# Interleaving the first batch's down tiles by halves of the contraction

## The chip, the cores and the metric

One core of one Trainium2 chip runs the whole program. The metric is the device time of that core in microseconds (us), lower is better. One run of a kernel has a profile; the other runs have a time and a mean granted clock alone (the share of full speed at which TensorE was let run). The times of a run are about 1.8 us longer than the span that its profile shows.

## The reference

```python
# q: 8 x 16 x 384 x 64, k and v: 8 x 4 x 384 x 64 (4 query heads share a key head)
attn = softmax(q @ k.T / sqrt(64)) @ v           # per batch and head
x = attn.transpose(0, 2, 1, 3).reshape(3072, 1024)
h = maximum(x @ w_in, 0)                         # w_in 1024 x 2048
out = (h * h) @ w_out                            # w_out 2048 x 1024, float32
```

The change touches only the last product, and of it only the 384 tokens of the first batch.

## The kernel before

The kernel works through 8 batches of 384 tokens. TensorE is given attention work of the next batch in between the feed-forward work of this one. A list scheduler, which runs when the kernel is built and has a clock of its own, fixes the order of the instructions on each engine. On the chip each engine then goes through its list in order and waits at semaphores.

The feed-forward has an "up" stage (x times w_in) and a "down" stage (times w_out). A down tile is 128 tokens by 512 output columns in one PSUM bank (6 or 7). Its contraction of 2048 is 16 matmuls of 512 columns, given out as four parts of 4. There are two column halves (`jj`) and three token blocks (`i3`), so six tiles a batch.

```python
    def load_w_out(jj, part):      # a quarter of w_out: column half jj, row half part
        R.add("gpsimd", lambda g: g.dma_start(
            w_out_sb[:, 8 * part:8 * part + 8, jj * 512:(jj + 1) * 512],
            moe_w_out[part * 1024:(part + 1) * 1024, jj * 512:(jj + 1) * 512]
            .rearrange("(c p) f -> p c f", p=128)),
            writes=[("w_out", jj, part)], dma=f"wo{jj}{part}", cost=5.3, issue=0.9)
    # ... (the eight loads of w_in are issued first, then:)
    for jj in range(2):
        for part in range(2):
            load_w_out(jj, part)
```

```python
    def ffn(b):
        # ... the up stage
        for jj in range(2):
            for i3 in range(NJ):                                     # NJ = 3
                # ... (the very last tile is cut in two)
                    at = []
                    for part in range(4):
                        yield down_part(b, jj, i3, c0, c1, part, at)

    def down_part(b, jj, i3, c0, c1, part, at):
        n = c1 - c0

        def piece():
            if part == 0:
                at.append(pick((6, 7)))
            i = at[0]

            def mm(pe):
                for c in range(4 * part, 4 * part + 4):
                    m = pe.matmul(bank(i)[:, 0:n], h2T[b % 2][:, c, i3 * 128:(i3 + 1) * 128],
                                  w_out_sb[:, c, c0:c1], start=(c == 0), stop=(c == NFC - 1))
                return m

            R.add("tensor", mm, reads=need, writes=[("bank", i)], cost=4 * (n / 2400 + 0.0025))
            # ... after part 3: DVE copies the bank to y_sb, SyncE stores it
        need = [("w_out", jj, part // 2)] + [("h2T", b % 2, c) for c in range(4 * part, 4 * part + 4)]
        return 0, need, (6, 7) if part == 0 else None, piece
```

Parts 0 and 1 need w_out's first row half, parts 2 and 3 its second. In the old order the second half is wanted after only 8 matmuls.

The softmax here doesn't subtract the row's maximum and nothing guards it: scores larger than these inputs give would overflow.

Of the kernel before, what the change touches and what calls it, by code (L numbers as in the profile page):

```python
# [136 lines left out]
def bass_gqa_attention__then__ffn_squared_relu_kernel(  # L137
# [13 lines left out]
    NJ = S // 128  # L151
# [38 lines left out]
    def bank(i):  # L190
        return ps[:, i, :]
# [4 lines left out]
    def pick(allowed):  # L196
        turn_count[0] += 1
        i = min(allowed, key=lambda i: (max(R.when(writes=[("bank", i)]), R.clock["tensor"]), used[i]))
        used[i] = turn_count[0]
        return i  # L200
# [226 lines left out]
    def up_part(b, c, at, k0, k1, banks=(6, 7)):  # L427
        def piece():
            if k0 == 0:
                at.append(pick(tuple(banks)))  # L430
                held.add(at[0])
            i = at[0]
            if k1 == NKC:
                held.discard(i)

            def mm(pe):
                for kc in range(k0, k1):
                    m = pe.matmul(bank(i)[:, 0:S], w_in_sb[:, kc, c * 128:(c + 1) * 128],  # L438
                                  xT[b % NXT][:, kc, :], start=(kc == 0), stop=(kc == NKC - 1))
                return m  # L440

            R.add("tensor", mm, reads=need, writes=[("bank", i)], cost=0.1625 * (k1 - k0))
            if k1 == NKC:
                r = hr_n[0] % NHR
                hr_n[0] += 1
                R.add("vector", lambda e: e.tensor_scalar_max(hr[r][:, :], bank(i)[:, 0:S], 0.0),  # L446
                      reads=[("bank", i)], writes=[("hr", r)], cost=0.48)
                R.add("scalar", lambda e: e.activation(h2T[b % 2][:, c, :], hr[r][:, :], AF.Square),  # L448
                      reads=[("hr", r)], writes=[("h2T", b % 2, c)], cost=0.42)

        need = [("w_in", c * 128 // WC)] + [("xT", b % NXT, kc) for kc in range(k0, k1)]
        return k1, need, banks if k0 == 0 else None, piece
# [10 lines left out]
    def ffn(b):  # L463

        for c in range(0 if b else EARLY, NFC):
            at = []
            for k0 in (0, 4):
                yield up_part(b, c, at, k0, k0 + 4)
        for jj in range(2):
            for i3 in range(NJ):  # L470
                last = b == B - 1 and (jj, i3) == (1, NJ - 1)
                for c0, c1 in ((512, 896), (896, 1024)) if last else ((512 * jj, 512 * jj + 512),):
# [19 lines that stand above are left out]
            if part == 3:  # L492
                yb = y_n[0] % (2 * NY)
                y_n[0] += 1
                ysl = y_sb[yb // 2][:, (yb % 2) * 512:(yb % 2) * 512 + n]
                R.add("vector", lambda e: e.tensor_copy(ysl, bank(i)[:, 0:n]),  # L496
                      reads=[("bank", i)], writes=[("y", yb)], cost=0.08 + n / 960)
                rows = out[b * S:(b + 1) * S, :].rearrange("(p j) f -> j p f", j=NJ)[i3]
                R.add("sync", lambda e: e.dma_start(rows[:, c0:c1], ysl),
                      reads=[("y", yb)], writes=[("out", b, i3, c0)], dma=f"y{yb}", cost=1.0)  # L500
                stored.append(("out", b, i3, c0))

        need = [("w_out", jj, part // 2)] + [("h2T", b % 2, c) for c in range(4 * part, 4 * part + 4)]
        return 0, need, (6, 7) if part == 0 else None, piece
# [90 lines left out]
    def feed():  # L595
        for b in range(B):
            for item in ffn(b):
                yield (b,) + item
# [9 lines left out]
    while av_q or av_open or sc_q or o_q or f_head is not None:  # L608
# [18 lines left out]
        if turn_q:  # L627
            b, g, w = turn_q[0]
# [5 lines left out]
        elif av_q:  # L634
            b, c = av_q[0]
# [5 lines left out]
        if sc_q:  # L641
            b, u = sc_q[0]
            if b == 0:
                tiles = {(0, x, t) for x, c0, n in smalls[u] for t in range(c0 // 128, (c0 + n) // 128)}
# [14 lines left out]
        for n, lane in enumerate(lanes):  # L659
            chunks, need, banks, _ = lane[0]  # L660
# [7 lines left out]
        if f_head is not None and not lanes:  # L668
            b, chunks, need, banks, piece = f_head
# [15 lines left out]
        if what[2] == "turn":  # L685
            b, g, w = turn_q.pop(0)
# [5 lines left out]
        elif what[2] == "av":  # L692
            b, c = av_q.pop(0)
            av_open = (b, c, av(b, c, spare))
            next(av_open[2])
        elif what[2] == "av2":
            b, c, rest = av_open
# [8 lines left out]
        elif what[2] == "o":  # L706
            b, c, _ = o_q.pop(0)
            turn_o_pe(b, c, spare)
            x_done[b] += 1
        elif what[2] == "sc":  # L710
            b, u = sc_q.pop(0)
# [44 lines left out]
```

## Time and profile before

The kernel takes 429.41 us (median of 3 runs, 429.10 to 429.62).

| of the profile before | |
|---|---|
| span | 427.2 us |
| TensorE busy | 421.9 us, 99% |
| second-busiest compute engine (ACT) | 194.2 us, 45% |
| TensorE waits on w_out | one, 1.1 us |

From the page of the kernel before (PE is TensorE, PEld its weight loads, DVE VectorE, ACT ScalarE, POOL GpSimd): busy time of TensorE with its share and instructions, the DMA busy tenths in 40 slices, the shares of the chain that ended last, the group of the down matmuls (busy us, mean ns of one, then idle time before them), and the loads of w_out (KB each, median us from issue to landing).

```profile
PE 421.9 (99%) x3462; PEld 231.6 (54%) x3462; DVE 157.9 (37%) x333; ACT 194.2 (45%) x194; POOL 55.2 (13%) x67
...
DMA  9999999999499469539919310063001100110012
...
PE 87%; DMA 10%; POOL 2%; issue 0%; DVE 0%; POOLq 0%
...
L487 PE MATMUL ps<-w_out_sb,h2T 128*128 128x512 bf16 (+2 forms) x784 | 172.3, 375 | 1.1 <-DMA w_out_sb<-in_moe_w_out_dram 1.1
...
w_out_sb<-in_moe_w_out_dram POOLq DMA_DIRECT2D x4, 1024.0 KB, 30.6
```

TensorE is the limit, so only its idle time can be won. The DMA engines are busy over 90% in the first ten slices (107 us), and the chain goes through DMA for 10% of the span. The chain is followed back from the end, so it meets the last wait before which TensorE depended on a transfer: the load of w_out.

All waits of TensorE in the kernel before (who, for what, us in total, times, longest):

```profile
PE ps L487 <- DMA w_out_sb<-in_moe_w_out_dram: 1.1, 1, 1.1
PE ps L545 <- DVE v_aug L540: 1.1, 1, 1.1
PE ps L309 <- DMA q_st<-in_q_dram: 0.4, 1, 0.4
PE ps L309 <- DVE qT L316: 0.2, 1, 0.2
```

L545 is the warm-up and L309 the turning of the first queries: start-up work. Only the first line is in the steady part. Its place is seen in the timeline of TensorE before (start us, us, engine, line, operation, what, count, and in brackets the idle time before it):

```profile
51.06 1.89 PE L487 MATMUL ps<-w_out_sb,h2T 128*128 128x512 bf16 x8
54.06 1.04 PE L487 MATMUL ps<-w_out_sb,h2T 128*128 128x512 bf16 x4 [1.11 <-DMA w_out_sb<-in_moe_w_out_dram]
54.94 1.28 PE L381 MATMUL ps<-v_aug,expT 128*128 128x65 bf16 x36
56.05 1.89 PE L487 MATMUL ps<-w_out_sb,h2T 128*128 128x512 bf16 x8
57.87 0.82 PE L356 MATMUL ps<-qT,kT 64*128 64x512 bf16 x8
...
76.17 5.36 PE L438 MATMUL ps<-xT,w_in_sb 128*128 128x384 bf16 x32
81.46 0.82 PE L356 MATMUL ps<-qT,kT 64*128 64x512 bf16 x8
```

Eight matmuls run (parts 0 and 1 of the first tile), then TensorE stands still until the second row half has landed. L381 is an attention-value group and L356 are scores of the next batch. A busy span's modelled end overhangs the start of the next matmul, so idle time is better counted from start to start: 8 matmuls at 0.216 us fill 51.06 to 52.79, and the next starts at 54.06. That is 1.27 us lost, a little more than the 1.11 in brackets.

### The profile page before, as it was taken

How to read it: one execution, taken by the hardware profiler on the slowest of the kernel's cores; microseconds unless marked ns; L12 is line 12 of the kernel's file. 1: busy time of each engine (PE TensorE's matmuls, PEld its weight loads, DVE VectorE, ACT ScalarE, POOL GpSimd, SP SyncE). 2: the span in 40 equal slices, each digit the busy share in tenths (PEclk: the TensorE clock that was granted, in tenths of full speed). 3: DMA queues.
4: the chain of work that ended last, by engine and by line, in shares of the span. 5: the costliest groups of instructions: out<-in, count | busy, mean ns of one | idle time of the engine just before them, and what ended most of it. 6: DMA issues, size and time to landing. Idle time of an engine off the chain costs nothing.

```text
span 427.2 us, 7835 instructions
## 1 busy us (share of the span) xinstructions
PE 421.9 (99%) x3462; PEld 231.6 (54%) x3462; DVE 157.9 (37%) x333; ACT 194.2 (45%) x194; POOL 55.2 (13%) x67
## 2 busy tenths in 40 slices
PE   8999999999999999999999999999999999999997
PEld 5665554555545555455554455555564465446544
DVE  3664332343423443234442244343441144214412
ACT  6957720477256773547745477732230033003300
POOL 8680001414012004004000000000000000000000
PEclk9999999999999999999999999999999999999999
DMA  9999999999499469539919310063001100110012
GB/s 172 194 186 201 185 202 217 201 174 151 92 201 164 32 130 123 126 88 153 106 45 180 87 45 18 2 104 93 27 2 49 74 26 1 51 74 26 1 66 82
DMA packets 96915, 44.30 MB, mean 104 GB/s; under 512 B 77296, under 2 KB 90864, under 8 KB 96880
## 3 DMA queue, kind: packets, MB, share of 16 engines
q0 software_dynamic: 36544, 17.44, 32.4%
q1 hardware_dynamic: 59664, 25.86, 29.5%
q8 instruction: 27, 0.44, 0.4%
q10 hardware_dynamic: 672, 0.49, 0.4%
q14 instruction: 8, 0.07, 0.0%
HBM read 35.65 MB, written 12.58 MB: 113 GB/s over the span
## 4 chain that ended last, share of the span: by engine, by line
PE 87%; DMA 10%; POOL 2%; issue 0%; DVE 0%; POOLq 0%
PE ps L487 39%; PE ps L438 35%; PE ps L381 7%; DMA w_out_sb<-in_moe_w_out_dram 7%; PE ps L356 7%; DMA v_st<-in_v_dram 4%; POOL q_st L237 1%; POOL w_in_sb L247 1%; POOL v_aug L269 0%; POOL w_out_sb L253 0%; DVE y_sb L496 0%; POOL ident L513 0%; POOL ident L512 0%; POOLq L513 0%; POOLq L741 0%
## 5 line engine op out<-in xcount | busy, mean ns | idle before, releaser
L438 PE MATMUL ps<-xT,w_in_sb 128*128 128x384 bf16 x1024 | 175.0, 326 | 0.0
L487 PE MATMUL ps<-w_out_sb,h2T 128*128 128x512 bf16 (+2 forms) x784 | 172.3, 375 | 1.1 <-DMA w_out_sb<-in_moe_w_out_dram 1.1
L366 ACT ACTIVATE expT<-ps 128x3072 bf16<-128x3072 f32 x42 | 114.4, 2724 | 64.6 <-PE ps L356 64.0
L438 PEld LDWEIGHTS ps<-xT,w_in_sb 128*128 128x128 bf16 x1024 | 97.1, 98 | 69.6 <-issue 6.2
L448 ACT ACTIVATE h2T<-hr 128x384 bf16<-128x384 f32 x128 | 64.3, 520 | 143.0 <-DVE hr L446 143.0
L487 PEld LDWEIGHTS ps<-w_out_sb,h2T 128*128 128x128 bf16 x784 | 73.6, 98 | 88.6 <-issue 5.1
L446 DVE TENSOR_SCALAR hr<-ps 128x384 f32<-128x384 f32 x128 | 71.3, 557 | 106.5 <-PE ps L438 106.5
L496 DVE COPY y_sb<-ps 128x512 f32<-128x512 f32 (+2 forms) x49 | 33.4, 681 | 124.0 <-PE ps L487 124.0
L381 PEld LDWEIGHTS ps<-v_aug,expT 128*128 128x128 bf16 x1152 | 39.9, 97 | 6.8 <-DVE rinv L390 0.5
L381 PE MATMUL ps<-v_aug,expT 128*128 128x65 bf16 x1152 | 41.8, 193 | 0.0
L396 DVE TENSOR_TENSOR o_sb<-ps,rinv 128x384 bf16<-128x384 f32 x64 | 35.7, 558 | 2.2
L356 PE MATMUL ps<-qT,kT 64*128 64x512 bf16 (+1 forms) x336 | 34.6, 325 | 0.0
L356 PEld LDWEIGHTS ps<-qT,kT 64*128 64x128 bf16 x336 | 13.0, 94 | 20.4 <-issue 5.7
L390 DVE RECIPROCAL rinv<-ps 128x6 f32<-128x6 f32 x64 | 12.2, 190 | 26.7 <-PE ps L381 26.7
L269 POOL COPY v_aug<-v_st 128x768 bf16<-128x768 bf16 x8 | 6.6, 828 | 86.7 <-PE ps L381 69.9
L345 ACT ACTIVATE expT<-ps 128x1024 bf16<-128x1024 f32 (+1 forms) x20 | 16.8, 991 | 1.0 <-PE ps L335 1.0
L264 POOL COPY k_dup<-k_st 128x1536 bf16<-128x1536 bf16 x7 | 10.3, 1467 | 42.3 <-DMA k_st<-in_k_dram 42.1
L237 POOL DMA_DIRECT2D q_st<-in_q_dram x17 | 14.9, 888 | 0.3 <-issue 0.2
L205 POOL DMA_DIRECT2D k_st<-in_k_dram x7 | 5.3, 764 | 37.9 <-DMA qT<-q_st 37.9
L335 PE MATMUL ps<-qT,kT 64*128 64x384 bf16 (+2 forms) x48 | 7.3, 334 | 0.1
L247 POOL DMA_DIRECT2D w_in_sb<-in_moe_w_in_dram x8 | 7.1, 900 | 0.0
L230 POOL DMA_DIRECT2D v_st<-in_v_dram x8 | 6.3, 789 | 0.0
(27 smaller groups left out, 41.9 us busy)
## 6 DMA issues: line engine op xcount, KB each, us to landing
out_dram<-y_sb SPq DMA_DIRECT2D x47, 256.0 KB, 2.0
q_st<-in_q_dram POOLq DMA_DIRECT2D x14, 384.0 KB, 8.6
w_in_sb<-in_moe_w_in_dram POOLq DMA_DIRECT2D x8, 512.0 KB, 14.6
w_out_sb<-in_moe_w_out_dram POOLq DMA_DIRECT2D x4, 1024.0 KB, 30.6
v_st<-in_v_dram POOLq DMA_DIRECT2D x8, 192.0 KB, 10.3
k_st<-in_k_dram POOLq DMA_DIRECT2D x7, 192.0 KB, 4.4
q_st<-in_q_dram POOLq DMA_DIRECT2D x3, 192.0 KB, 6.1
xT<-o_sb SPq DMA_TRANSPOSE x28, 3.9
```

What stands on the lines that cost most here:

```text
L237: R.add("gpsimd", lambda g: g.dma_start(q_st[st][:, h0:h1, :], q[b, h0:h1].rearrange("h (p j) d -> p h (j d)", j=NJ)), writes=[("q_st", st ...
L345: R.add("scalar", lambda e: e.activation(dst, src, AF.Exp, scale=0.125), reads=keys, writes=[("expT", (b * NU + u) % NEX, t) for u, _, _ i ...
L356: m = pe.matmul(flat[:, k0 * HC + c0:k0 * HC + c1], kT[b % 2][64 * x:64 * x + 64, u + k0, :], q_cols(b, (u + k0) // NJ, x, c0, c1))
L366: R.add("scalar", lambda e: e.activation(dst, src, AF.Exp, scale=0.125), reads=keys, writes=[("expT", (n + m) % NEX, t) for m in range(2) ...
L381: m = pe.matmul(po[:, f - 6 * s2, 0:D + 1], w, v_aug[b % 2][:, g * NJ + j, 0:D + 1], start=(j == 0), stop=(j == NJ - 1))
L390: R.add("vector", lambda e: e.reciprocal(rinv[r].ap().unsqueeze(2), po[:, :, D:D + 1]), reads=[("bank", i)], writes=[("rinv", r)], cost=0.13)
L396: R.add("vector", lambda e: e.tensor_tensor(dst, srcv, rbv, ALU.mult), reads=[("bank", i), ("rinv", r)], writes=[("o_sb", o, s2)], cost=0.48)
L438: m = pe.matmul(bank(i)[:, 0:S], w_in_sb[:, kc, c * 128:(c + 1) * 128], xT[b % NXT][:, kc, :], start=(kc == 0), stop=(kc == NKC - 1))
L446: R.add("vector", lambda e: e.tensor_scalar_max(hr[r][:, :], bank(i)[:, 0:S], 0.0), reads=[("bank", i)], writes=[("hr", r)], cost=0.48)
L448: R.add("scalar", lambda e: e.activation(h2T[b % 2][:, c, :], hr[r][:, :], AF.Square), reads=[("hr", r)], writes=[("h2T", b % 2, c)], cost ...
L487: m = pe.matmul(bank(i)[:, 0:n], h2T[b % 2][:, c, i3 * 128:(i3 + 1) * 128], w_out_sb[:, c, c0:c1], start=(c == 0), stop=(c == NFC - 1))
L496: R.add("vector", lambda e: e.tensor_copy(ysl, bank(i)[:, 0:n]), reads=[("bank", i)], writes=[("y", yb)], cost=0.08 + n / 960)
```

## The change

The intent is to read w_out's second row half later. In batch 0 token blocks 0 and 1 first do their parts 0 and 1, in two banks, and then their parts 2 and 3. Block 2 follows alone. Sixteen down matmuls then stand before the first read of the second half. No instruction is added or removed, and batches 1 to 7 keep their code.

```diff
-        for jj in range(2):
+        for jj in range(2 if b == 0 else 0):
+            ats = [[] for _ in range(NJ)]
+            for tiles in ((0, 1), (2,)):
+                for half in range(2):
+                    for i3 in tiles:
+                        for part in (2 * half, 2 * half + 1):
+                            yield down_part(b, jj, i3, 512 * jj, 512 * jj + 512, part, ats[i3])
+        for jj in range(2 if b else 0):
```

## The prediction

> **What bounds the kernel now.** TensorE. The busy table gives PE 421.9 of 427.2 us (99%) at full granted clock; ACT 45%, DVE 37%. Matmuls stream: late in the chain view 96 down matmuls of 512 columns take 20.72 us, 216 ns each. The Trainium skill ("TensorE: Matmul & The Clock Gate", "Back-to-back issue gap") gives 512 columns at 2.4 GHz plus 2.5 ns, also 216 ns; the trace agrees. So only PE idle time can be won. The waits view filtered to PE has four waits: 1.1, 0.4 and 0.2 us in the lead-in, and one later: 1.1 us of the down matmuls on w_out.
>
> **That wait.** In the PE timeline batch 0's down tiles begin at 51.06 us with eight matmuls (parts 0 and 1 of tile 0, on w_out's first row half). The third part, on the second half, starts at 54.06 us. The four w_out loads, issued at 24.8 to 27.4 us, land 23.1, 28.4, 32.9 and 38.2 us later: at about 47.9, 54.0, 59.4 and 65.6 us, one per 5.7 us, behind each other on DMA engines that the page shows over 90% busy. Eight matmuls fill their slots until 51.06 + 1.73 = 52.79 us. Lost, start to start: 1.27 us (the view shows 1.1, as a modelled end overhangs its slot).
>
> **What the change does.** No instruction is added or removed. In batch 0 come parts 0 and 1 of tiles 0 and 1, then parts 2 and 3 of both, then tile 2. Sixteen matmuls (3.46 us) precede the first read of the second half, so it comes no sooner than 54.5 us, and 1.1 us later if an attention-value group (36 matmuls, 1.12 us) falls between, as one now does after the third part. Slack after landing: 0.4 to 1.5 us. The wait should vanish.
>
> In the second column half nothing is to be gained: its second row half is now read at about 67.5 us, 1.9 us after landing.
>
> **Costs.** Two banks are open at once, so an eviction (0.69 us) must fit into the other tile's two parts (1.73 us). It does, closely if DVE has an attention group too (about 1.3 us). The first store comes 1.7 us later, with no reader.
>
> **Does the gain survive?** After 54 us PE never waits in the trace, so the saving goes through unless a DMA becomes the limit. The nearest: batch 2's first scores start at 81.46 us; their query transpose, issued at 72.30, landed 7.8 us later, about 80.1. Shifted, the scores start at 80.2: just in time; a few tenths may be lost.
>
> **Prediction.** 429.4 - 1.27 = about 428.2 us (0.3%); 8 in 10 between 427.7 and 429.0. Faster by over 2%: 1%; within 2%: 98%; slower by over 2%: 1%.
>
> **What would show it right.** No PE wait on w_out; the first second-half matmul at 54.5 to 56 us; batch 1's first up matmuls at about 74.9 us instead of 76.17; the last down group 1.27 us earlier (404.16 to 402.9); PE busy time unchanged; w_out landings unchanged within 0.5 us.
>
> **What would make it wrong.** A new PE wait: on the query transpose at batch 2's first scores, on an eviction when a bank is reused, or still on w_out if it lands later than in the recorded run. The order of later work is fixed at build time by a list scheduler with its own clock, so a moved tile can reshuffle attention work of batches 1 and 2 and make or remove waits of about 1 us. A bank chosen wrongly there would show as a wrong result, not as time.

## The result, and the profile after

| | median us | range | runs |
|---|---|---|---|
| before, same rounds | 429.25 | 428.53 to 429.75 | 6 |
| after | 427.84 | 427.56 to 427.95 | 6 |

The ratio is 0.9966 with a 95% interval of 0.9953 to 0.9979: a gain of 0.34%, small but clear of noise. A ratio is always the mean time of one kernel's fast runs over that of the other's of the same rounds, so it is not quite the ratio of the medians. The output is correct. The runs after also lie closer together: 0.39 us from end to end against 1.22 us.

From the page after, the lines that answer to those of before:

```profile
PE 422.2 (99%) x3462; PEld 231.9 (54%) x3462; DVE 157.9 (37%) x333; ACT 194.4 (46%) x194; POOL 55.2 (13%) x67
...
DMA  9999999999989369449829310053001100110012
...
PE 97%; DMA 1%; DVE 0%; ACT 0%; issue 0%; POOL 0%; POOLq 0%
...
L494 PE MATMUL ps<-w_out_sb,h2T 128*128 128x512 bf16 (+2 forms) x784 | 172.1, 375 | 0.0
...
w_out_sb<-in_moe_w_out_dram POOLq DMA_DIRECT2D x4, 1024.0 KB, 30.8
```

The work is the same (the down matmuls are now L494; the 0.3 us more of TensorE busy time lie in the first 10 us, 8.60 against 8.30, before anything that the change touches). The idle time before them went from 1.1 to 0.0, and the chain no longer passes through the load: its DMA share fell from 10% to 1%. Such a share is not the size of a gain. The chain had 10% on DMA, and removing that wait gave 0.34%, because behind it stood TensorE work that was nearly as long.

All waits of TensorE after:

```profile
PE ps L552 <- DVE v_aug L547: 1.1, 1, 1.1
PE ps L309 <- DVE qT L316: 0.2, 1, 0.2
```

The timeline of TensorE after:

```profile
51.08 2.75 PE L494 MATMUL ps<-w_out_sb,h2T 128*128 128x512 bf16 x12
53.67 1.28 PE L381 MATMUL ps<-v_aug,expT 128*128 128x65 bf16 x36
54.78 1.89 PE L494 MATMUL ps<-w_out_sb,h2T 128*128 128x512 bf16 x8
56.60 0.82 PE L356 MATMUL ps<-qT,kT 64*128 64x512 bf16 x8
...
74.90 5.36 PE L438 MATMUL ps<-xT,w_in_sb 128*128 128x384 bf16 x32
80.28 0.82 PE L356 MATMUL ps<-qT,kT 64*128 64x512 bf16 x8
```

The sequence of kinds and counts is the same: 12 down matmuls, an attention-value group, 8 down matmuls, scores. On every engine the two kernels' lists have the same instructions in the same order by shape. Only which tile and part a down matmul belongs to has changed, so the scheduler has not reshuffled anything. The first read of the second half is now the second four of the eight at 54.78, at 55.65 us. The next up stage begins 1.27 us earlier (76.17 to 74.90), as much as the idle time that was removed (the down stage itself began 0.02 us later). At the scores of batch 2 the distance from there is 5.29 us before and 5.38 after: 0.09 us were given back (0.01 in the profile of the next series, 75.02 to 80.32). The weight loads there now have a wait of 0.4 us on the transposed queries, which landed at 80.24. This is the line of the waits view after:

```profile
PEld ps L356 <- DMA qT<-q_st: 0.4, 1, 0.4
```

The gain then stays to the end. The last piece of down matmuls in the chain, first before, then after:

```profile
404.16 20.77 PE ps L487 x112
```

```profile
402.98 20.77 PE ps L494 x112
```

That is 1.18 us, which is 1.27 less 0.09.

### The profile page after: what moved, and what is told of

It reads as the page before. It is cut to its first block, busy times and chain, and to the rows that moved or that the text cites. A ratio compares the mean times of both kernels' runs of the same rounds, so it can differ in the third digit from the quotient of the medians.

```text
span 426.0 us, 7835 instructions
## 1 busy us (share of the span) xinstructions
PE 422.2 (99%) x3462; PEld 231.9 (54%) x3462; DVE 157.9 (37%) x333; ACT 194.4 (46%) x194; POOL 55.2 (13%) x67
## 4 chain that ended last, share of the span: by engine, by line
PE 97%; DMA 1%; DVE 0%; ACT 0%; issue 0%; POOL 0%; POOLq 0%
PE ps L438 40%; PE ps L494 39%; PE ps L381 9%; PE ps L356 7%; DMA q_st<-in_q_dram 1%; PE ps L335 1%; PE ps L309 1%; PE ps L414 0%; PE ps L292 0%; ACT expT L345 0%; DVE qT L316 0%; DVE y_sb L503 0%; POOL ident L520 0%; POOL ident L519 0%; POOLq L520 0%
## 5 line engine op out<-in xcount | busy, mean ns | idle before, releaser
L494 PE MATMUL ps<-w_out_sb,h2T 128*128 128x512 bf16 (+2 forms) x784 | 172.1, 375 | 0.0
L494 PEld LDWEIGHTS ps<-w_out_sb,h2T 128*128 128x128 bf16 x784 | 73.7, 98 | 87.2 <-issue 5.1
```

## The experiments

Theory W: the gain is the wait for w_out's second row half and nothing else. Rival V: it is the new order as such (two banks in turn, evictions and stores spaced differently). In all the kernels below the lists of all engines except GpSimd are the same by shape as before, so that only the named thing differs. The exception is the pair with the early key load, in which SyncE's list differs too (the key transpose comes one store earlier); the two kernels of that pair have the same lists as each other. Edits of kernels in the new order are shown against the changed kernel, the others against the kernel before.

The table has the places that decide, from each trace: when w_out's second part (second row half of column half 0) and fourth part (of column half 1) landed, and when the first matmul that needs it started.

| kernel | 2nd part landed | read | 4th part landed | read |
|---|---|---|---|---|
| before | 54.02 | 54.06 | 65.59 | 67.53 |
| after | 54.85 | 55.65 | 67.11 | 67.99 |
| after, again | 54.95 | 55.77 | 67.20 | 68.12 |
| only column half 0 | 54.93 | 55.82 | 66.34 | 66.44 |
| only column half 1 | 54.87 | 54.91 | 66.05 | 70.12 |
| no wait, wrong data | 54.54 | (58.06) | 66.99 | 67.04 |
| one part between | 54.00 | 54.89 | 65.97 | 67.24 |

Where a read stands some 0.05 us after a landing, TensorE was waiting for it. (In the kernel with wrong data the first tile doesn't read the second part; 58.06 is the first read of it, by the second tile.)

### The change again

No edit.

> The changed kernel again, as the mark for the other runs of this chip. Theory W (the gain is the wait for w_out's second row half, and nothing else): 1.0 to 1.8 us under the kernel before, near 427.8, no PE wait on w_out. Rival V (the gain is the new order as such: two banks alternating, evictions and stores spaced otherwise): the same here.

Measured: 427.63 us (427.51 to 427.89, 5 runs) against 429.55 (428.82 to 430.33, 11 runs) of the kernel before on this chip, ratio 0.9960 (0.9948 to 0.9972). No wait on w_out. The gain is confirmed, here 1.9 us between the medians.

### Only column half 0

```diff
-        for jj in range(2 if b == 0 else 0):
+        for jj in range(1 if b == 0 else 0):
...
-        for jj in range(2 if b else 0):
+        for jj in range(0 if b else 1, 2):
```

> Only the first column half is interleaved. W: all of the gain, within 0.3 us of the changed kernel (427.8), no PE wait on w_out; the second column half's reads come after their landings anyway. V: about half of the gain, near 428.5.

Measured: 427.94 us, ratio 0.9973 (0.9957 to 0.9988), 6 runs from 427.71 to 429.45. By the median W holds. But two runs stand apart, at 428.30 and 429.45, where the whole change has none above 427.95. In the profiled run the fourth part landed at 66.34 and was read at 66.44: no wait of the matmuls (a weight load ahead of them waited 0.3 us for it), but only 0.1 us of room.

### Only column half 1

```diff
         for jj in range(2 if b == 0 else 0):
+            if jj == 0:
+                for i3 in range(NJ):
+                    at = []
+                    for part in range(4):
+                        yield down_part(b, jj, i3, 0, 512, part, at)
+                continue
```

> Only the second column half is interleaved. W: nothing gained, within 0.4 us of the kernel before (429.2), the PE wait of 1 to 2 us on w_out still there near 53 us. V: about half of the gain, near 428.5, too.

Measured: 429.58 us (428.90 to 431.67, 6 runs), ratio 1.0011 (0.9993 to 1.0028). Nothing gained, as W has it and V hasn't. The wait is still there, and longer than in the first profile, since the half landed at 54.87 in this run and not at 54.02. The waits view of this kernel has:

```profile
PE ps L500 <- DMA w_out_sb<-in_moe_w_out_dram: 1.8, 1, 1.8
```

### The old order without the wait

Parts 2 and 3 of the very first tile read the first row half, which has long landed. Its output is wrong, which doesn't matter for the time.

```diff
+        back = 8 if (b, jj, i3) == (0, 0, 0) and part >= 2 else 0
...
-                                  w_out_sb[:, c, c0:c1], start=(c == 0), stop=(c == NFC - 1))
+                                  w_out_sb[:, c - back, c0:c1], start=(c == 0), stop=(c == NFC - 1))
...
-        need = [("w_out", jj, part // 2)] + ...
+        need = [("w_out", jj, 0 if back else part // 2)] + ...
```

> The old order, but the third and fourth part of the very first down tile read w_out's first row half (long landed) in place of the second: wrong on purpose in one tile, all else as before, the order on every engine the same. W: the whole gain without any interleaving, 427.7 to 428.0, within 0.3 us of the changed kernel, no PE wait on w_out. V: no gain, 429.2.

Measured: 427.89 us, ratio 0.9973 (0.9959 to 0.9988), 5 runs: 427.75, 427.83, 427.89, 428.58, 429.20. By the median the whole gain comes with no interleaving at all, which V rules out. By the mean it is less, 0.27% against the 0.40% of the change on the same chip, since two of the five runs stand apart. The expectation of no wait on w_out was a miss, though. The profile is that of the run of 428.58, and its timeline has a new wait:

```profile
61.78 4.48 PE L488 MATMUL ps<-w_out_sb,h2T 128*128 128x512 bf16 x20
67.04 8.81 PE L488 MATMUL ps<-w_out_sb,h2T 128*128 128x512 bf16 x40 [0.78 <-DMA w_out_sb<-in_moe_w_out_dram]
```

This is the second column half: its fourth part landed at 66.99, and with the first wait gone TensorE came to it at 66.1. So the wait that the change takes away had hidden a second one behind it. The pair with a late fourth part, further down, goes into this; that it is what slowed the run of 429.20 too is not shown, as that run has no profile.

### The half made late, old order

The second and third load swap places. The scheduler's own costs are set so that it gives out the same order.

```diff
-    for jj in range(2):
-        for part in range(2):
+    for part in range(2):
+        for jj in range(2):
             load_w_out(jj, part)
...
-dma=f"wo{jj}{part}", cost=5.3, issue=0.9)
+dma=f"wo{jj}{part}", cost=(5.3, 5.3, 0.0, 10.6)[2 * jj + part], issue=0.9)
```

> Old order, the loads of w_out's second row half (first column half) and first row half (second column half) issued in swapped order, so that the half in question lands one load later, at about 59.4 to 60 us in place of 54 to 54.8. W: the wait grows by one load, 5.7 us: 434.9 us, a PE wait of about 7 us. V (order as such, waits no matter): about 429.2 plus a small part of that.

### The half made late, new order

The same edit on the changed kernel.

> New order with the same swapped loads. W: the read now comes before the landing in this order too, so a wait comes back, of about 59.8 - 55.6 = 4 us, and the time is about 432. Against the swapped old order the gain must be the TensorE work that the change puts ahead of the read: 8 matmuls (1.73 us), or 2.85 us if the attention-value group of 1.12 us also moves ahead of it, as the trace after has it: I expect 2.85. V: the gain stays 1.4 us.

Measured: 436.19 us (435.65 to 437.85) for the old order and 433.52 (432.86 to 433.96) for the new, 4 runs each, on the same chip. Between them lie 2.7 us of the medians (3.0 of the means), where W expected 2.85 and V 1.4. The two profiled runs lie only 1.7 us apart, but there the half landed 1.02 us later in the new order (60.20 against 59.18). Counted from the landing to the start of the last part of batch 0's down stage, it is 22.70 us in the old order and 20.03 in the new, again 2.67 us. So the advantage of the order is not a fixed amount. It is the TensorE work put ahead of the read (8 matmuls, 1.73 us, and the attention-value group, 1.12), as far as the landing is late enough to use it up. With the loads in their usual order the landing is only 1.1 to 2.1 us later than an unhindered TensorE would have come to it (in the seven profiles of the table), and that is what is gained.

The wait of the old order was a little shorter than the expected 7 us (6.3), yet the times are 1.3 and 1.5 us longer than W expected. The stretches of the old-order run show why (window, its length, busy us and count of PE, PEld, DVE, ACT and POOL, then the granted clock, the DMA share, which adds up the times of all packets and so can pass 1, and GB/s):

```profile
51.00:54.00 3.00, 1.96 (x10) 0.69 (x8) 0.56 (x1) 2.66 (x2) 0.00 (x0) 1.00 1.21 196
54.00:59.00 5.00, 0.00 (x0) 0.00 (x0) 0.00 (x0) 0.00 (x0) 0.00 (x0) 0.64 1.24 204
59.00:61.00 2.00, 1.78 (x6) 0.68 (x7) 0.00 (x0) 0.00 (x0) 0.00 (x0) 0.50 1.25 209
61.00:63.00 2.00, 2.00 (x39) 1.82 (x38) 0.83 (x3) 0.00 (x0) 0.00 (x0) 0.68 1.26 206
63.00:65.00 2.00, 2.00 (x16) 0.80 (x13) 1.28 (x3) 0.00 (x0) 0.00 (x0) 1.00 1.54 190
```

During the long wait the granted clock falls to half (it is 1.00 from 52.9 to 55.4 us, 0.50 from 55.5 to 62.2, and 1.00 from 62.3 on) and stays there for a while after work resumes. The timeline of this run shows the price in the work itself:

```profile
59.22 1.89 PE L487 MATMUL ps<-w_out_sb,h2T 128*128 128x512 bf16 x4 [6.26 <-DMA w_out_sb<-in_moe_w_out_dram]
60.90 1.89 PE L381 MATMUL ps<-v_aug,expT 128*128 128x65 bf16 x36
62.62 1.89 PE L487 MATMUL ps<-w_out_sb,h2T 128*128 128x512 bf16 x8
```

From 59.22 to 62.62 are 3.40 us; the same two groups took 56.05 - 54.06 = 1.99 before. So this wait cost 1.41 us more than its own length. The new-order run has a shorter wait:

```profile
55.14 1.02 PE L494 MATMUL ps<-w_out_sb,h2T 128*128 128x512 bf16 x4
60.24 1.68 PE L494 MATMUL ps<-w_out_sb,h2T 128*128 128x512 bf16 x4 [4.08 <-DMA w_out_sb<-in_moe_w_out_dram]
```

There the way from the delayed matmul to the part after next took 4.19 us (60.24 to 64.43) against 2.58 in the changed kernel (55.65 to 58.23): 1.6 us more. The Trainium skill ("TensorE: Matmul & The Clock Gate", "What's actually happening") states that the array falls to half its clock after an idle window of about 3.4 us and needs as long a busy one to recover. The recovery in these two runs is near that: the clock was back 3.05 and 3.67 us after work resumed. The fall fits in one run only. In the new order it came 4.3 us after the end of the last matmul (56.17 to 60.49), when work had already gone on for 0.25 us, but in the old order 2.5 us after it (52.96 to 55.45), sooner than such a window.

The waits of 0.8 to 2.3 us in the other profiled runs left the mean clock at 1.00. But five runs without a profile have a mean clock of 0.996, and each is 2.0 to 2.5 us above the median of its kernel's other runs: 432.03 and 431.89 of the kernel before (one of 11 in each of two later series), 431.67 of "only column half 1", and 432.11 and 432.33 of the kernel with the early key load and only column half 0 interleaved. All are kernels whose profile shows a wait of 1.1 to 2.3 us on w_out. The kernels without such a wait (the change, the smaller loads, half the interleaving) have no such run. So a shorter wait, too, now and then seems to cost more than its length; where the clock fell in these runs is not on record.

### Smaller loads, old order

```diff
-            w_out_sb[:, 8 * part:8 * part + 8, jj * 512:(jj + 1) * 512],
-            moe_w_out[part * 1024:(part + 1) * 1024, jj * 512:(jj + 1) * 512]
+            w_out_sb[:, 4 * part:4 * part + 4, jj * 512:(jj + 1) * 512],
+            moe_w_out[part * 512:(part + 1) * 512, jj * 512:(jj + 1) * 512]
...
-        for part in range(2):
+        for part in range(4):
             load_w_out(jj, part)
...
-        need = [("w_out", jj, part // 2)] + ...
+        need = [("w_out", jj, part)] + ...
```

The cost that the scheduler counts for a load is halved too.

> Old order, but each w_out load split in two by rows (8 loads of 512 KB), each part of a tile waiting for its own quarter. W: the third quarter lands about 2.9 us before the fourth, near 51.2 us, ahead of its read at 52.8; the fourth near 54 to 54.8, its read near 54.8. So nearly the whole gain without touching the matmuls: 427.8 to 428.3, PE waits on w_out of 0 to 0.3 us. V: no gain, 429.2.

Measured: 427.99 us (427.62 to 428.27, 6 runs), ratio 0.9961 (0.9942 to 0.9981), no TensorE wait on w_out. The third quarter landed at 51.00 and was read at 52.78. The fourth landed at 54.74 and was read at 54.88, where an unhindered TensorE would have come at 52.78 + 0.86 + 1.12 = 54.76 (one part, one attention-value group): 0.1 us lost. W holds: a smaller load gains as much as another order.

### Half the interleaving

```diff
-            for tiles in ((0, 1), (2,)):
-                for half in range(2):
-                    ...
+            for i3, part in ((0, 0), (0, 1), (1, 0), (0, 2), (0, 3), (1, 1), (1, 2), (1, 3),
+                             (2, 0), (2, 1), (2, 2), (2, 3)):
+                yield down_part(b, jj, i3, 512 * jj, 512 * jj + 512, part, ats[i3])
```

> In the new order only one part (4 matmuls) of tile 1 goes between the first and the second half of tile 0, where the change puts two. W: the second half is read at about 51.06 + 2.59 + 1.12 = 54.8 us, as it lands (54.0 to 54.8): 427.8 to 428.3, a PE wait of 0 to 0.4 us. V: a smaller gain, in proportion to the interleaving, near 428.5.

Measured: 427.82 us (427.51 to 428.06, 6 runs), ratio 0.9958 (0.9938 to 0.9977), no wait on w_out. Four matmuls gain as much as eight, against V. The second half was read at 54.89 us, about where expected, and in the profiled run it had landed at 54.00. Among the other profiles it landed as late as 54.95, so what is left here is next to no room: half the interleaving is enough, but only just.

### A late fourth part, with and without the second interleaving

The key load of batch 2, which follows w_out otherwise, is issued just ahead of w_out's fourth part. This was done to "only column half 0" and to the whole change.

```diff
         for part in range(2):
+            if (jj, part) == (1, 1):
+                load_k(2)
             load_w_out(jj, part)
...
-            load_k(loaded, after)
+            if loaded != 2:
+                load_k(loaded, after)
```

> Only the first column half interleaved, and the key load of batch 2 (192 KB, it followed w_out before) issued just ahead of w_out's fourth part, which so lands 1.1 to 1.4 us later, at 67.4 to 68.5 us; what follows lands as before. Theory I (interleaving the second column half is an insurance against a late fourth part): its second half is read at 66.3 to 66.4 us here, so a PE wait of 1.0 to 2.1 us on w_out comes, 428.8 to 429.9. Rival N, my prediction's sentence (nothing to be gained in the second column half): no wait, 427.8.

> The whole change with the same early key load. I: the read comes at 68.0 to 68.1 us, so a wait of 0 to 0.4 us, 427.7 to 428.2, and 1 to 1.7 us under the run with only the first column half interleaved. N: no difference between the two.

Measured: 430.81 us (430.00 to 432.33, 6 runs) with only column half 0 interleaved, and 429.44 (428.86 to 429.96, 6 runs) with the whole change. The fourth part landed at 68.46 and 69.59 in the two profiled runs, later than I had reckoned, so both wait and both absolute expectations were too low. The timelines, the first of them that of the kernel with only column half 0:

```profile
68.50 8.81 PE L494 MATMUL ps<-w_out_sb,h2T 128*128 128x512 bf16 x40 [2.32 <-DMA w_out_sb<-in_moe_w_out_dram]
```

```profile
69.64 7.08 PE L494 MATMUL ps<-w_out_sb,h2T 128*128 128x512 bf16 x32 [1.80 <-DMA w_out_sb<-in_moe_w_out_dram]
```

The two kernels are told apart all the same: 1.4 us of the medians (1.6 of the means), within the 1 to 1.7 that theory I expected, where N expected none. Part of this is the clock: two of the six runs with only column half 0 are those at 0.996, and without them its median is 430.09, 0.65 us above the whole change. The profiles are the better evidence. There the fourth part landed 1.13 us later with the whole change, and the times are still 0.4 us apart in its favour. From that landing to the start of the last part of batch 0's down stage it is 7.82 us with only column half 0 and 6.10 with the whole change. The 1.72 us between them are the 8 matmuls (1.73 us) that the second interleaving puts ahead, as the wait before 32 matmuls instead of 40 shows. So interleaving the second column half does nothing while the fourth part is in time, and saves up to 1.73 us when it is late. That what follows would land as before was also a miss: the queries of batch 2 landed at 80.99 and 81.94 us, against 80.24 in the changed kernel.

### Both remedies

The smaller loads on the changed kernel.

> The change and the quarter loads together. If theory W holds, all waits on w_out are gone with either, so there is nothing left to win: 427.5 to 428.0, no more than 0.2 us from the changed kernel, TensorE waits only in the lead-in.

Measured: 427.74 us (427.43 to 428.58, 6 runs), against 427.63 to 427.84 of the change in its own two series. The profile is that of the run of 428.30: no wait on w_out, but 1.2 us of waits for the first queries in the lead-in. Nothing is left to be won at this place. No kernel beats the change by more than the runs scatter.

## Why the prediction was right

The predicted time was 428.2 us, the measured one 427.84, inside the range of 427.7 to 429.0, and both the place and the way were as predicted.

- **TensorE is the limit, and one wait is to be won.** Right. The wait went away, and the next up stage began 1.27 us earlier (74.90). Taking the wait away without interleaving gained the same by the median, and interleaving only where the wait was not gained nothing. This is shown.
- **The size, 1.27 us.** A little low: the medians differ by 1.41 and, in the second series, 1.92. The 1.27 is one run's wait, and the wait varies with the landing. Among the profiles the second part landed from 54.00 to 54.95. Started at 51.26, as in the kernel with only column half 1 interleaved, TensorE would have gone on at 52.99 and did at 54.91: 1.92 us lost. That the scatter of the kernel before comes from this is consistent with the narrower scatter after, but it is argued: the runs without a profile have no landing.
- **Slack of 0.4 to 1.5 us.** Right in its range. The read came at 55.65, 0.80 after the landing. My w_out landings "unchanged within 0.5 us" were not: 54.85 against 54.02 for the second, 67.11 against 65.59 for the fourth, with the same loads in the same order. Of the 0.83 us of the second, 0.55 are that it was issued later (26.17 against 25.62).
- **The second column half: nothing to be gained.** This step failed. It was read from one trace, in which the fourth part had 1.9 us of room, and the room had two parts that don't last. The change itself takes 1.27 us of it, and the landing varies by more than the rest (65.59 to 67.20). In the profiled run of the change the fourth part landed at 67.11. Without the second interleaving TensorE would have come to it at 66.27 and waited 0.84 us (worked out from its read at 67.99, since parts are 0.86 us apart and the read would be two of them sooner). The run with wrong data shows such a wait, 0.78 us, and the pair with the early key load shows the second interleaving at work.
- **The scores of batch 2 "just in time; a few tenths may be lost".** Right: 0.09 us of TensorE time, with the queries landing at 80.24 and the scores at 80.28.
- **Bank reuse.** Right: no new TensorE wait on an eviction. Two accumulations are open at once here. The Trainium skill ("PSUM — Partial Sum Buffer", "The four PSUM rules") warns that of two groups open at once in one bank the second to start makes the first lose its partial sum, without an error. No run here tries it. The code keeps them apart only because the bank choice finds the other bank free by the scheduler's clock. The correct results of every run with right data show that it did.

## What to carry to other kernels

When one engine is busy 99% of the time, look for the few waits it has left, count each from start to start, and move independent work ahead of the late operand: the gain is the smaller of the wait and the work moved, unless a later wait takes its place, as in the kernel with wrong data. Before trusting the room that another operand has in one trace, subtract the time that you are about to save and compare what is left with how much its landing varies between runs. Smaller loads with a semaphore each can do the same as another order of work.

## What the Trainium skill lacked or had wrong

- "TensorE: Matmul & The Clock Gate", "Back-to-back issue gap", gives about 131 ns a matmul as the sustained figure at 512 columns for a stream of weight loads and matmuls, and 216 ns as the isolated gap that would be too high there. Here such a stream, with a weight load for every matmul, has 216 ns: 96 matmuls of 512 columns in 20.72 us. The formula given for the isolated case is the one that holds.
- The same page, "HAM oscillation — how this bites in real kernels", reckons for its example kernel about 1.67 us at the lower clock after each long wait, of which half is the penalty. That is no rule for other kernels: here a single wait cost 1.4 us more than its length after one of 6.3 us, and 1.6 us after one of 4.1.
- The same page, "What's actually happening", gives at least one idle window of about 3.4 us as what halves the clock. Here it fell 2.5 us after the last matmul in one run, sooner than that (4.3 us after it in another), and five runs of kernels whose profiled waits are 1.1 to 2.3 us have a mean clock of 0.996.
- None of the pages that I read says how much the landing of a load queued behind others varies from run to run. Here the same 1 MB load, with nothing changed in the queue ahead of it, was issued between 27.36 and 28.35 us and landed between 65.59 and 67.20 us in seven profiles, 38.0 to 39.4 us after its issue, and the one two places ahead of it between 54.00 and 54.95.
